# Batched attention and MLP mixer: the last 64 tokens of u with swapped operands, and two transposes moved to ScalarE's queue

## The chip, the core and the metric

The kernel runs on one core of a Trainium2 chip. A core has a matrix engine (TensorE, PE in the tables; PEld is its weight load), VectorE (DVE), ScalarE (ACT), GpSimd (POOL) and SyncE (SP), which here only issues transfers. Each engine works through its own list of instructions in order, and waits on semaphores for the others and for transfers. The time is that of the device in microseconds, from the program's start to its end, lower is better. The profile's span runs from the first to the last recorded instruction and is 1.8 us shorter here.

## The reference

Eight batches, each attention followed by a two-stage mixer:

```python
scores = scale * np.matmul(q, k.transpose(0, 1, 3, 2))        # 8 heads, 576 tokens, 64 wide
scores = np.where(masks[None, :, :, :], scores, -1000000000.0)
...
x = np.ascontiguousarray(attn_out.transpose(0, 2, 1, 3)).reshape(B, S, H * D)
...
xt = x.transpose(0, 2, 1)
h = np.maximum(xt @ w_tok1, 0.0) @ w_tok2
u = x + h.transpose(0, 2, 1)
h2 = np.maximum(u @ w_ch1, 0.0) @ w_ch2
return (u + h2).astype(np.float32)
```

Heads 0 to 3 see the last 32 tokens, heads 4 to 7 every fourth of the last 128, so that scores are computed in bands. x has 576 tokens by 512 channels; the token stage goes 576 to 256 to 576, the channel stage 512 to 1536 to 512. 576 is four blocks of 128 tokens and a tail of 64, and the change is about the tail.

## The kernel before

The loop over batches (L1167) makes one iteration a batch. In iteration b the generator `gen_main(b)` emits the channel stage of batch b, and between its pieces `interleave` (L975) puts a list of steps, sorted by a time that is written by hand beside each: t is advanced by the costs that the pieces and steps give, and a step is emitted when its time is reached. The order in which instructions are emitted is the order on each engine; nothing is reordered later. The steps of iteration b are, for batch b + 1, the last attention products (`value_steps`, matmuls av, VectorE scales them into xn = x), the token stage's hidden layer (`mix_steps`, tiles h1, written `h` in the tables) and u; for batch b + 2 the scores and their exponentials on ScalarE (attp, attd, attt; two groups of heads, group 0 and group 1, `scores_twin`, exponentials L547), their masks on GpSimd, and the transposes of q and k by DMA from SP (tt, kr, qt; L353); for batch b + 3 the loads on SP (L192, L198, later the v loads).

The main line: `gp` matmuls (L934) of u's transpose with the first channel weights, relu by ScalarE into `gt`; then `gen_out`, which makes the output products yx and yw (L778) by a seven-product scheme, with sums of gt tiles on VectorE (`gate_sums`, L737), adds u (`with_u`, L793) and further products (`with_t`, L798), and stores. Batches are paired for their tails: the 64 tail tokens of an even batch and of the odd batch after it share one tile of 128 and are worked through in the odd iteration (`gp_tails`, gt L925; `tails` in `gen_out`, L744 to L755).

u has four forms from batch 2 on. Its blocks of 128 tokens are made in iteration b - 1 by `emit_u` (L640): matmuls of w_tok2's columns with h1 and an add of x on VectorE (L655). A DMA transpose from SP, `uT_dma` (L702), turns all four blocks into utm. ScalarE copies the second half of that into utd in natural order (`uT_place`, L863), for the gp matmuls. Late in iteration b a second DMA transpose, `u_natural` (L708, u<-utd), turns utd back over into u's second half, which `with_u` needs for the last products. The tail is made by `emit_u(b, 4)` (L659 to L664): two matmuls of 128x512 of which only 64 rows are used, and an add of 64x512 into u16t; in odd batches from 3 on another transpose from SP turns the pair of tails over into utt (L700).

PSUM banks are handed out by name, three "fl", three "main" and two "sc", each in turn; a matmul into a bank waits for the reader of what was in it before. Transfers issued from SP and ScalarE are counted on eight lanes of semaphores (DMAHW0 to DMAHW7) in rotation: a transfer that waits for a lane raises the same lane when it has landed.

Of the kernel before, what the change touches and what calls it, by code (L numbers as in the profile page):

```python
# [68 lines left out]
def kernel(  # L69
# [90 lines left out]
    uTt = fixed("utt", [128, 4, 128])  # L160
# [129 lines left out]
    xn, u16w, uT, uT0 = {}, {}, {}, {}  # L290
    gta = fixed("gt", [128, NMB, GW])
    u16t = [fixed(f"u16t{i}", [128, 4, 128]) for i in range(2)] * 2
# [347 lines left out]
    def emit_u(b, s, h1):  # L640
# [15 lines left out]
        else:  # L656
# [6 lines left out]
            t = u16t[b // 2]  # L663
            nc.vector.tensor_tensor(out=t[rows], in0=blocks4(p[rows]), in1=blocks4(xn[b][rows, 4]), op=ALU.add)  # L664

    def emit_uT(b, cb):
        odd = b % 2
        p = bank("fl" if cb % 2 == (cb > 1 if b else 0) else "main", 3, f"tpu_{b}_{cb}", FP16)
# [8 lines left out]
        if cb < 2:  # L677
# [3 lines left out]
            if odd:  # L681
                nc.tensor.transpose(out=p[:, 0:128], in_=u16t[b // 2][:, cb], identity=ident)
            copy(eng, t, p[:, 0:512 + m0])
        else:
# [4 lines left out]
            if odd:  # L689
                nc.tensor.transpose(out=grid[:, :, 0:32], in_=u16t[b // 2][:, cb], identity=perm)  # L690
# [3 lines left out]
    def turned(b):  # L694
        return b >= 2

    def uT_dma(b, tail):
        i = b % 2
        if tail:
            nc.sync.dma_start_transpose(out=uTt, in_=u16t[b // 2].rearrange("p x c -> p (x c)"))  # L700
        else:
            nc.sync.dma_start_transpose(out=uTm[i].rearrange("p x s t -> p (x s) t"),  # L702
                                        in_=u16w[b].rearrange("p x s c -> p (x s c)"))

    def u_natural(b):
        u = u16w[b]
        if turned(b):
            nc.sync.dma_start_transpose(out=u[:, 2:4].rearrange("p x s c -> p (x s) c"),  # L708
                                        in_=uTd.rearrange("p x t -> p (x t)"))
            return  # L710
# [28 lines left out]
    def gen_out(b):  # L739
# [4 lines left out]
        def tails():  # L744
# [7 lines left out]
            nc.vector.tensor_tensor(out=blocks4(o32), in0=blocks4(p), in1=u16t[b // 2], op=ALU.add)  # L752
# [6 lines left out]
        gate_sums(b, 1, (2, 1, 4) if ahead else (2,))  # L759
        if odd and not last:  # L760
# [3 lines left out]
            yield from tail  # L764
        else:
# [90 lines left out]
    def uT_place(b, cb):  # L856
        i = b % 2
        tail = uTt[:, cb]
# [36 lines left out]
    def mix_steps(b, t_h1, t_h1b, t_u, t_uT, du=1.0, turn=6.0, gap=2.6):  # L895
        h1 = [sb.tile([128, DM], FP16, tag="h1", bufs=4, name=f"h1_{b}_{jb}") for jb in range(2)]
# [4 lines left out]
        for i, s in enumerate((4, 0, 1, 2, 3)):  # L901
            steps.append((t_u + du * i, 0.44, lambda s=s: emit_u(b, s, h1)))
        if turned(b):
            for t, tail in ((turn, False), (turn + 1.0, True))[:1 + b % 2]:
                steps.append((t_u + t * du, 0.0, lambda tail=tail: uT_dma(b, tail)))
# [7 lines left out]
    def gen_main(b):  # L913
# [17 lines left out]
        for mb in range(NMB):  # L931
# [13 lines left out]
            if b and mb == (11 if b == 1 else 10):  # L945
                gate_sums(b, 0, (2, 1, 4) if odd and b + 1 < B else (2, 1))
# [153 lines left out]
    def u_half(s, half):  # L1100
# [3 lines left out]
        t = (u16t[0] if s == 4 else u16(0, s))[:, 2 * half:2 * half + 2]  # L1104
# [146 lines left out]
```

## Time and profile before

| | before |
|---|---|
| median of 3 runs | 278.54 us (277.87 to 278.73) |
| the profiled execution: its time | 278.42 us |
| the profiled execution: span | 276.6 us |
| DMA moved | 55.50 MB, mean 201 GB/s |
| DMA transposes, us to landing: kr, qt | 3.6, 3.4 |
| DMA transposes, us to landing: tt, utm | 4.3, 4.6 |
| DMA transposes, us to landing: u<-utd, utt | 3.8, 2.8 |

All times to landing are medians from issue. In the page, a line of section 5 gives the source line, engine, operation, tiles and their sizes, the count, then busy time, mean duration in ns and the idle time ahead of it with what ended it. In the list of waits a row names who waited, for whom, the sum in us, how often, and the longest. In a timeline a row gives the start, the duration, engine, line, operation and tiles, and how many instructions stand together; a bracket holds the idle time ahead of it and who ended it; an engine with a q behind it (SPq, ACTq) is its queue issuing transfers. Iteration 2 ends near 130 us, iteration 4 near 190 and iteration 5 near 222.

### The profile page before, as it was taken

Reading aid. Unit: us, or ns where it says so; the run is one execution under the profiler, and the core shown is the slowest. Engines: PE = TensorE matmul, PEld = TensorE weight load, DVE = VectorE, ACT = ScalarE, POOL = GpSimd, SP = SyncE. Lnnn points to the kernel's source line nnn. Section 1 sums busy time; section 2 is a strip of 40 time slices with the busy share of each in tenths; the row PEclk is TensorE's granted clock in tenths of the full one; section 3 lists DMA queues with packets and bytes.
Section 4 is the critical chain, followed back from the end, with each engine's and each line's share of the span. In section 5 each row is a group of like instructions: output and inputs, shape, how many; then the busy total and the mean of one; then the engine's idle time right before and its main releaser. Section 6 shows DMA issues by size and latency. Waiting matters only on the chain.

```text
span 276.6 us, 6790 instructions
## 1 busy us (share of the span) xinstructions
PE 265.8 (96%) x2694; PEld 197.2 (71%) x2694; DVE 168.3 (61%) x340; ACT 149.0 (54%) x291; POOL 158.8 (57%) x214
## 2 busy tenths in 40 slices
PE   6899999999999999997999999999999999999994
PEld 2796676897666876685775876687776866786673
DVE  6767668575568655674649454775475473961363
ACT  2864774363674465467545656476546565236500
POOL 7880760389858759849973589739980870000000
PEclk9999999999999999999999999999999999999999
DMA  7999999995979799999999999989999220553015
GB/s 216 271 248 238 291 241 210 316 241 159 343 132 226 151 316 281 233 165 259 304 221 186 257 280 255 172 156 316 304 211 148 81 79 2 99 147 78 0 40 152
DMA packets 116783, 55.50 MB, mean 201 GB/s; under 512 B 84976, under 2 KB 115696, under 8 KB 116752
## 3 DMA queue, kind: packets, MB, share of 16 engines
q1 hardware_dynamic: 112096, 49.63, 75.9%
q0 software_dynamic: 2640, 3.94, 7.9%
q10 hardware_dynamic: 2016, 1.51, 1.8%
q8 instruction: 21, 0.34, 0.5%
q14 instruction: 10, 0.08, 0.1%
HBM read 38.12 MB, written 9.44 MB: 172 GB/s over the span
## 4 chain that ended last, share of the span: by engine, by line
PE 85%; DMA 7%; DVE 4%; issue 1%; ACT 1%; ACTq 0%; POOL 0%; DVEq 0%
PE gp L934 29%; PE yx L778 12%; PE yw L778 9%; PE h1p L637 5%; PE up L649 4%; PE gt L925 4%; PE yp L961 4%; PE yp L747 3%; DMA lt<-in_k_dram 3%; PE sc L522 3%; DMA u<-utd 2%; DMA w1p<-in_moe_w_tok_dram 2%; PE h1p L635 1%; PE av L614 1%; PE av L619 1%; DVE gt L737 1%
## 5 line engine op out<-in xcount | busy, mean ns | idle before, releaser
L109 ACT ACTIVATE gt<-gp 128x512 f16<-128x512 f32 x89 | 53.2, 598 | 50.4 <-PE gp L934 50.1
L778 PEld LDWEIGHTS <-gt 128*128 128x128 f16 x600 | 57.0, 98 | 10.2 <-issue 2.0
L934 PE MATMUL gp<-utd,w 128*128 128x512 f16 x144 | 54.7, 380 | 0.0
L934 PE MATMUL gp<-utm,w 128*128 128x512 f16 x144 | 54.6, 379 | 0.0
L934 PEld LDWEIGHTS <-w 128*128 128x128 f16 x384 | 39.1, 113 | 19.8 <-issue 0.5
L115 POOL TENSOR_TENSOR attp<-attp,const 128x1280 f16<-128x1280 f16 x12 | 31.6, 2637 | 23.4 <-ACT attp L547 23.4
L737 DVE TENSOR_TENSOR gt<-gt 128x768 f16<-128x768 f16 x56 | 32.2, 605 | 12.5 <-ACT gt L109 12.2
L115 DVE TENSOR_TENSOR xn<-av,rec 128x320 f16<-128x320 f32 x64 | 31.4, 491 | 2.2
L115 POOL TENSOR_TENSOR attd<-attd,const 128x1024 f16<-128x1024 f16 x12 | 25.5, 2124 | 7.7 <-issue 5.4
L934 PE MATMUL gp<-uT,w 128*128 128x512 f16 x96 | 25.8, 380 | 0.0
L793 DVE TENSOR_TENSOR o<-yx,u 128x512 f32<-128x512 f32 x22 | 15.2, 689 | 11.2 <-PE yx L778 10.5
L778 PE MATMUL yx<-w,gt 128*128 128x256 f16 x168 | 20.6, 273 | 0.0
L778 PE MATMUL yx<-wsum_a,gt 128*128 128x256 f16 x168 | 20.6, 273 | 0.0
L547 ACT ACTIVATE attp<-sc 128x480 f16<-128x480 f32 (+1 forms) x36 | 15.9, 538 | 8.7 <-PE sc L522 8.7
L655 DVE TENSOR_TENSOR u<-up,xn 128x512 f16<-128x512 f32 x26 | 17.8, 688 | 4.1 <-PE up L649 4.1
L626 DVE RECIPROCAL rec<-av 128x5 f32<-128x5 f32 x64 | 12.2, 191 | 12.2 <-PE av L623 12.1
L105 POOL CAST c_k<-l_k 128x512 f16<-128x512 f32 x29 | 17.6, 616 | 2.2 <-DMA l_k<-in_k_dram 1.3
L863 ACT COPY utd<-utm 128x512 f16<-128x512 f16 x12 | 12.7, 1129 | 10.3 <-DMA u<-utd 6.6
L105 POOL CAST c_q<-l_q 128x512 f16<-128x512 f32 x26 | 16.3, 630 | 2.9 <-DMA l_q<-in_q_dram 2.2
L664 DVE TENSOR_TENSOR u16t<-up,xn 64x512 f16<-64x512 f32 x7 | 4.8, 689 | 21.0 <-PE up L660 21.0
L109 ACT ACTIVATE h<-h1p 128x256 f16<-128x256 f32 x31 | 11.8, 384 | 8.9 <-PE h1p L637 8.4
L798 DVE TENSOR_TENSOR o<-yw,o 128x512 f32<-128x512 f32 x13 | 9.0, 691 | 11.4 <-PE yw L778 11.3
(158 smaller groups left out, 549.6 us busy)
## 6 DMA issues: line engine op xcount, KB each, us to landing
l_q<-in_q_dram SPq DMA_DIRECT2D x15, 512.0 KB, 6.6
l_k<-in_k_dram SPq DMA_DIRECT2D x14, 512.0 KB, 7.4
out_dram<-o SPq DMA_DIRECT2D x26, 256.0 KB, 4.1
l_vn<-in_v_dram SPq DMA_DIRECT2D x32, 128.0 KB, 6.7
l_vd<-in_v_dram SPq DMA_DIRECT2D x16, 256.0 KB, 4.2
w<-in_moe_w_ch_dram POOLq DMA_DIRECT2D x6, 512.0 KB, 7.6
out_dram<-o SPq DMA_DIRECT2D x17, 128.0 KB, 2.7
l_vt<-in_v_dram SPq DMA_DIRECT2D x8, 256.0 KB, 4.7
```

What stands on the lines that cost most here:

```text
L105: eng.tensor_copy(out=out, in_=in_)
L109: nc.scalar.activation(out=out, in_=in_, func=AF.Relu)
L115: eng.tensor_tensor(out=out, in0=x, in1=y, op=ALU.mult)
L547: nc.scalar.activation(out=out, in_=in_, func=AF.Exp, scale=0.125)
L626: nc.vector.reciprocal(out=rec[:, :, 0], in_=av[:, :, 64])
L637: nc.tensor.matmul(out=p, lhsT=w[:, s, j], rhs=x[:, s, c], start=False, stop=(s == 3))
L655: nc.vector.tensor_tensor(out=u16(b, s), in0=blocks4(p), in1=blocks4(xn[b][:, s]), op=ALU.add)
L737: nc.vector.tensor_tensor(out=out, in0=x, in1=y, op=op)
L778: nc.tensor.matmul(out=p, lhsT=gta[:, k0 + mb, r:r + 128], rhs=weights[:, mb, c], start=(first and not mb and (not a or len(parts) > 2)), ...
L793: nc.vector.tensor_tensor(out=grid(o[(i, j)]), in0=grid(p), in1=u, op=ALU.add)
L863: nc.scalar.copy(out=natural(uTd[:, cb - 2]), in_=uTm[i][:, cb].rearrange("p r m -> p m r"))
L934: nc.tensor.matmul(out=p, lhsT=w3_block(cb, mb), rhs=uT[(b, cb)][0], start=(i == 0), stop=(i == 3))
```

## The change

From batch 2 on the tail of u is no longer made in iteration b - 1 but in iteration b, at t = 1.6, by a new function `emit_u_tail`. It swaps the operands: h1 is the stationary side and the 64 columns of w_tok2 the moving one, so that the result is already transposed: four blocks of 128 channels by 64 tokens, eight matmuls of 128x64 and one add of 128x256. The add needs x's last block transposed, xtt, which a DMA transpose from ScalarE's queue makes in iteration b - 1 (`turn_x`). In odd batches SP turns the pair of tails over into u16t at t = 2.6 (`turn_tails`), the other way round than before; there are two utt and one u16t now.

The transpose u<-utd of batches 2 to 5 is issued from ScalarE's queue at t = 17.3 (19.7 in odd iterations) in place of SP's at 14.6 (15.0); in batches 6 and 7 it stays. `uT_dma` comes 1.0 steps of u earlier relative to u's blocks. In batch 1 one transposed tile takes a bank "fl" in place of "main" (`emit_uT`), and gate sum 4 stands behind the add of the tails in iterations 1, 3 and 5 (group 1) and 1 (group 0).

```diff
--- before.py
+++ after.py
@@ -157,7 +157,8 @@
     w4 = [w4a[:, i] for i in range(NMB)]
     idle = fixed("idle", [128, 512])
     uTm = [fixed(f"utm{i}", [128, 4, 4, 128]) for i in range(2)]
-    uTt = fixed("utt", [128, 4, 128])
+    uTt = [fixed(f"utt{i}", [128, 4, 128]) for i in range(2)]
+    xTt = fixed("xtt", [128, 4, 128])
     uTd = fixed("utd", [128, 2, 512])
 
     def emit_fixed():
@@ -287,9 +288,9 @@
         return steps
 
 
-    xn, u16w, uT, uT0 = {}, {}, {}, {}
+    xn, u16w, uT, uT0, h1s = {}, {}, {}, {}, {}
     gta = fixed("gt", [128, NMB, GW])
-    u16t = [fixed(f"u16t{i}", [128, 4, 128]) for i in range(2)] * 2
+    u16t = fixed("u16t", [128, 4, 128])
 
     def u16(b, s):
         if b not in u16w:
@@ -660,12 +661,12 @@
                 nc.tensor.matmul(out=p, lhsT=w2[jb][:, c0:c0 + 128], rhs=h1[jb],
                                  start=(jb == 0), stop=(jb == 1))
             rows = slice(64, 128) if odd else slice(0, 64)
-            t = u16t[b // 2]
+            t = u16t
             nc.vector.tensor_tensor(out=t[rows], in0=blocks4(p[rows]), in1=blocks4(xn[b][rows, 4]), op=ALU.add)
 
     def emit_uT(b, cb):
         odd = b % 2
-        p = bank("fl" if cb % 2 == (cb > 1 if b else 0) else "main", 3, f"tpu_{b}_{cb}", FP16)
+        p = bank("fl" if (cb != 2 if b else cb % 2 == 0) else "main", 3, f"tpu_{b}_{cb}", FP16)
         if odd:
             t = sb.tile([128, 640], FP16, tag="ut1", bufs=4, name=f"uT_{b}_{cb}")
         else:
@@ -679,7 +680,7 @@
                 nc.tensor.transpose(out=p[:, m0 + 128 * s:m0 + 128 * s + 128],
                                     in_=u16(b, s)[:, cb], identity=ident)
             if odd:
-                nc.tensor.transpose(out=p[:, 0:128], in_=u16t[b // 2][:, cb], identity=ident)
+                nc.tensor.transpose(out=p[:, 0:128], in_=u16t[:, cb], identity=ident)
             copy(eng, t, p[:, 0:512 + m0])
         else:
             grid = p[:, 0:4 * RS].rearrange("p (r i) -> p r i", i=RS)
@@ -687,25 +688,37 @@
             for s in range(4):
                 nc.tensor.transpose(out=grid[:, s, m0:m0 + 128], in_=u16(b, s)[:, cb], identity=ident)
             if odd:
-                nc.tensor.transpose(out=grid[:, :, 0:32], in_=u16t[b // 2][:, cb], identity=perm)
+                nc.tensor.transpose(out=grid[:, :, 0:32], in_=u16t[:, cb], identity=perm)
             copy(eng, natural(t), grid[:, :, 0:128 + m0].rearrange("p r m -> p m r"))
         uT[(b, cb)] = (t[:, 128:640], t[:, 0:128]) if odd else (t, None)
 
     def turned(b):
         return b >= 2
 
-    def uT_dma(b, tail):
+    def uT_dma(b):
         i = b % 2
-        if tail:
-            nc.sync.dma_start_transpose(out=uTt, in_=u16t[b // 2].rearrange("p x c -> p (x c)"))
-        else:
-            nc.sync.dma_start_transpose(out=uTm[i].rearrange("p x s t -> p (x s) t"),
-                                        in_=u16w[b].rearrange("p x s c -> p (x s c)"))
-
-    def u_natural(b):
+        nc.sync.dma_start_transpose(out=uTm[i].rearrange("p x s t -> p (x s) t"),
+                                    in_=u16w[b].rearrange("p x s c -> p (x s c)"))
+
+    def turn_x(b):
+        nc.scalar.dma_start_transpose(out=xTt, in_=xn[b][:, 4])
+
+    def turn_tails(b):
+        nc.sync.dma_start_transpose(out=u16t, in_=uTt[b // 2 % 2].rearrange("p x t -> p (x t)"))
+
+    def emit_u_tail(b):
+        p = bank("fl", 3, f"up_{b}_4")[:, 0:256].rearrange("p (x t) -> p x t", t=64)
+        for cb in range(4):
+            for jb in range(2):
+                nc.tensor.matmul(out=p[:, cb], lhsT=h1s[b][jb][:, 128 * cb:128 * cb + 128], rhs=w2[jb][:, 512:S],
+                                 start=(jb == 0), stop=(jb == 1))
+        t = slice(64 * (b % 2), 64 * (b % 2) + 64)
+        nc.vector.tensor_tensor(out=uTt[b // 2 % 2][:, :, t], in0=p, in1=xTt[:, :, t], op=ALU.add)
+
+    def u_natural(b, queue=nc.sync):
         u = u16w[b]
         if turned(b):
-            nc.sync.dma_start_transpose(out=u[:, 2:4].rearrange("p x s c -> p (x s) c"),
+            queue.dma_start_transpose(out=u[:, 2:4].rearrange("p x s c -> p (x s) c"),
                                         in_=uTd.rearrange("p x t -> p (x t)"))
             return
         for cb in (2, 3):
@@ -749,19 +762,22 @@
                 if mb in (3, 7):
                     yield 0.87
             o32 = sb.tile([128, DM], FP32, tag="o32", bufs=4, name=f"o32_{b}_4")
-            nc.vector.tensor_tensor(out=blocks4(o32), in0=blocks4(p), in1=u16t[b // 2], op=ALU.add)
+            nc.vector.tensor_tensor(out=blocks4(o32), in0=blocks4(p), in1=u16t, op=ALU.add)
             nc.sync.dma_start(out=out[b - 1, 512:S, :], in_=o32[0:64])
             nc.sync.dma_start(out=out[b, 512:S, :], in_=o32[64:128])
             yield 0.87
 
         base = turn["main"]
         ahead = odd and not last
-        gate_sums(b, 1, (2, 1, 4) if ahead else (2,))
+        gate_sums(b, 1, (2, 1) if ahead else (2,))
         if odd and not last:
             tail = tails()
             yield next(tail)
             spare.append(base)
             yield from tail
+            if b == 1:
+                gate_sums(b, 0, (4,))
+            gate_sums(b, 1, (4,))
         else:
             spare.append(base)
         turn["main"] = base + 2
@@ -855,7 +871,7 @@
 
     def uT_place(b, cb):
         i = b % 2
-        tail = uTt[:, cb]
+        tail = uTt[b // 2 % 2][:, cb]
         if cb < 2:
             uT[(b, cb)] = (uTm[i][:, cb].rearrange("p s t -> p (s t)"), tail)
         else:
@@ -893,16 +909,15 @@
         return steps
 
     def mix_steps(b, t_h1, t_h1b, t_u, t_uT, du=1.0, turn=6.0, gap=2.6):
-        h1 = [sb.tile([128, DM], FP16, tag="h1", bufs=4, name=f"h1_{b}_{jb}") for jb in range(2)]
+        h1 = h1s[b] = [sb.tile([128, DM], FP16, tag="h1", bufs=4, name=f"h1_{b}_{jb}") for jb in range(2)]
         steps = []
         for half, at in ((0, t_h1), (1, t_h1b)):
             for jb in range(2):
                 steps.append((at + 0.9 * jb, 0.55, lambda jb=jb, half=half: emit_h1(b, jb, half, h1[jb])))
-        for i, s in enumerate((4, 0, 1, 2, 3)):
+        for i, s in enumerate((0, 1, 2, 3) if turned(b) else (4, 0, 1, 2, 3)):
             steps.append((t_u + du * i, 0.44, lambda s=s: emit_u(b, s, h1)))
         if turned(b):
-            for t, tail in ((turn, False), (turn + 1.0, True))[:1 + b % 2]:
-                steps.append((t_u + t * du, 0.0, lambda tail=tail: uT_dma(b, tail)))
+            steps.append((t_u + turn * du, 0.0, lambda: uT_dma(b)))
             for t, cb in ((0.0, 2), (0.0, 0), (gap, 3), (gap, 1)):
                 steps.append((t_uT + t, 0.0, lambda cb=cb: uT_place(b, cb)))
         else:
@@ -943,7 +958,7 @@
                 for g in range(2):
                     gate_sums(b, g, (3,))
             if b and mb == (11 if b == 1 else 10):
-                gate_sums(b, 0, (2, 1, 4) if odd and b + 1 < B else (2, 1))
+                gate_sums(b, 0, (2, 1, 4) if odd and 1 < b < B - 1 else (2, 1))
         if b:
             yield from gen_out(b)
             return
@@ -1181,11 +1196,11 @@
             steps += scores2[:10]
             steps += at(34.0, 0.0, [lambda: emit_loads_qk(3)])
         elif b == 1:
-            steps += at(13.5, 0.0, [lambda: u_natural(1)])
+            steps += at(13.5, 0.0, [lambda: u_natural(1)]) + at(24.0, 0.0, [lambda: turn_x(2)])
             va = value_steps(2, 0.0, 1.0)
             steps += [(0.8 + 0.4 * i, c, f) for i, (_, c, f) in enumerate(scores2[10:])]
             steps += [(t, c, f) for t, (_, c, f) in zip((2.2, 3.0, 4.8, 5.6, 8.2, 9.0, 10.4, 11.2), va)]
-            steps += mix_steps(2, 7.0, 13.0, 15.1, 24.6, 1.0, 5.6, 0.8)
+            steps += mix_steps(2, 7.0, 13.0, 15.6, 24.6, 1.0, 5.1, 0.8)
             casts = cast_steps(3)
             steps += [(6.0 + 0.5 * i, 0.0, casts[i]) for i in (0, 2, 4, 6, 8)]
             steps += [(9.5 + 1.0 * i, 0.0, lambda i=i: cast_qk(3, "q", i, nc.scalar)) for i in range(4)]
@@ -1204,12 +1219,19 @@
             steps += at(11.0, 0.3, casts[9:14]) + at(12.5, 0.0, [places[i] for i in (0, 1, 4)])
             steps += at(13.0, 0.3, casts[14:16]) + at(14.0, 0.0, places[2:4]) + at(14.2, 0.0, casts[16:])
         else:
-            late = 2.4 * (b % 2)
-            steps += at(14.6 + late / 6, 0.0, [lambda b=b: u_natural(b)])
+            odd = b % 2
+            late = 2.4 * odd
+            if b + 1 < B:
+                steps += at(23.2 if odd else 20.4, 0.0, [lambda b=b: turn_x(b + 1)])
+            steps += at(1.6, 0.25, [lambda b=b: emit_u_tail(b)])
+            if odd:
+                steps += at(2.6, 0.0, [lambda b=b: turn_tails(b)])
+            steps += at(14.6 + late / 6 if b + 2 >= B else 17.3 + late, 0.0,
+                        [lambda b=b: u_natural(b, nc.sync if b + 2 >= B else nc.scalar)])
             if b + 1 < B:
                 va = value_steps(b + 1, 0.4, 0.95)
                 steps += va[:6] + [(t + late / 5, c, f) for t, c, f in va[6:]] + mix_steps(
-                    b + 1, 5.4 + late / 6, 8.2 + late / 6, 10.6 + late / 6, 22.4 + late, 0.9, 4.1, 1.0)
+                    b + 1, 5.4 + late / 6, 8.2 + late / 6, 10.6 + late / 6, 22.4 + late, 0.9, 3.1, 1.0)
             if b + 2 < B:
                 steps += at(2.0, 0.6, cast_steps(b + 2)) + score_steps(b + 2, 21.4 if b % 2 else 18.0, 8.4 if b % 2 else 6.4)
                 places = place_steps(b + 2)
```

Three places in the order of the program follow, before and after. A row has the source line, the operation, tile written and tiles read, size, and the semaphores that it waits for; PE_49, DVE_49, Pool_49 and Activation_49 are the engines' own.

The first is ScalarE in iteration 2, from the copy of k's last part (kt) to the copies into utd; sc_0 are the scores of group 0. Before:

```order
L103 COPY kt<-kr 128x512 [waits DMAHW7_49,Pool_49]
L547 ACTIVATE attp<-sc_0_5_2193 128x2x128 [waits PE_49,Activation_49,Pool_49]
L547 ACTIVATE attt<-sc_0_5_2193 128x2x64 [waits Activation_49]
...
L547 ACTIVATE attp<-sc_0_4_2192 128x2x128 [waits Activation_49]
L547 ACTIVATE attt<-sc_0_4_2192 128x2x64 [waits Activation_49]
L863 COPY utd<-utm_90 128x512 [waits DMAHW4_49,DMAHW3_49,Activation_49]
```

and with the change:

```order
L103 COPY kt<-kr 128x512 [waits DMAHW0_49,Pool_49]
L721 DMA_TRANSPOSE u_2_1640<-utd 128x8x128 [waits DMAHW4_49,DMAHW3_49,DMAHW6_49,DMAHW2_49,DMAHW7_49,DMAHW1_49,Activation_49]
L548 ACTIVATE attp<-sc_0_5_2196 128x2x128 [waits PE_49,Pool_49]
L548 ACTIVATE attt<-sc_0_5_2196 128x2x64
...
L548 ACTIVATE attp<-sc_0_4_2195 128x2x128
L548 ACTIVATE attt<-sc_0_4_2195 128x2x64
L704 DMA_TRANSPOSE xtt<-xn_1904 128x4x128 [waits DMAHW5_49,DVE_49]
L879 COPY utd<-utm_90 128x512 [waits DMAHW6_49]
```

Two transposes have come into the queue, one ahead of group 0's exponentials and one ahead of the copies. The first of them waits for lanes 1, 2, 3, 4, 6 and 7.

The second is SP in the same iteration, from the transposes of batch 4's k and q to batch 5's loads. Before:

```order
L353 DMA_TRANSPOSE kr<-c_k_1962 128x8x128 [waits DMAHW7_49,Pool_49]
L353 DMA_TRANSPOSE qt<-c_q_1957 128x8x128 [waits DMAHW0_49]
L353 DMA_TRANSPOSE kr<-c_k_1962 128x8x128 [waits DMAHW1_49,Pool_49]
L353 DMA_TRANSPOSE qt<-c_q_1957 128x8x128 [waits DMAHW2_49]
L702 DMA_TRANSPOSE utm_90<-u_3_2104 128x16x128 [waits DMAHW3_49,DVE_49]
L708 DMA_TRANSPOSE u_2_1643<-utd 128x8x128 [waits DMAHW4_49,Activation_49]
L700 DMA_TRANSPOSE utt<-u16t_95 128x4x128 [waits DMAHW5_49]
L198 DMA lt_2176<-in_q_dram 64x8x64 [waits DMAHW6_49]
```

and with the change:

```order
L354 DMA_TRANSPOSE kr<-c_k_1970 128x8x128 [waits DMAHW0_49,Pool_49]
L354 DMA_TRANSPOSE qt<-c_q_1965 128x8x128 [waits DMAHW1_49]
L354 DMA_TRANSPOSE kr<-c_k_1970 128x8x128 [waits DMAHW2_49,Pool_49]
L354 DMA_TRANSPOSE qt<-c_q_1965 128x8x128 [waits DMAHW3_49]
L700 DMA_TRANSPOSE utm_90<-u_3_2102 128x16x128 [waits DMAHW4_49,DVE_49]
L199 DMA lt_2189<-in_q_dram 64x8x64 [waits DMAHW5_49]
L199 DMA lt_2189<-in_k_dram 64x8x64 [waits DMAHW7_49]
```

Two transposes behind utm are gone, and lt comes next. The lanes of kr, qt, kr, qt and utm are now 0 to 4; lanes 1 to 4 are among those for which ScalarE's u<-utd waits, at the values that these very transfers raise, and lane 7 is that of tt just ahead of them.

The third is PE with the tail, up_4. Before, that of batch 3 in iteration 2, between gp_7 and gp_8:

```order
L934 LDWEIGHTS w_1_85
L934 MATMUL gp_7_2082<-utm_89,w_1_85 128x512
L660 LDWEIGHTS w_81
L660 MATMUL up_4_2089<-h_3_0_1901,w_81 128x512
L660 LDWEIGHTS w_81
L660 MATMUL up_4_2089<-h_3_1_1902,w_81 128x512
L934 LDWEIGHTS w_2_86
L934 MATMUL gp_8_2096<-utd,w_2_86 128x512
```

and with the change that of batch 2 in the same iteration, behind the second head's values matmuls:

```order
L624 LDWEIGHTS attt
L624 MATMUL av_1_1923<-vv_70,attt 128x65
L713 LDWEIGHTS h_2_0_1317
L713 MATMUL up_4_1935<-w_81,h_2_0_1317 128x64
L713 LDWEIGHTS h_2_1_1318
L713 MATMUL up_4_1935<-w_81,h_2_1_1318 128x64
...
L949 LDWEIGHTS w_0_84
L949 MATMUL gp_1_1920<-utd,w_0_84 128x512
```

Batch 3's two matmuls of 512 columns have gone from iteration 2 (its tail comes in iteration 3), and batch 2's eight of 64 columns, of which two are shown, have come to its start; before, batch 2's tail stood in iteration 1.

More of the change, by code (lines that the diff above doesn't have):

```diff
@@ L1103, in u_half @@
         rows = slice(0, 64) if s == 4 else slice(0, 128)
-        t = (u16t[0] if s == 4 else u16(0, s))[:, 2 * half:2 * half + 2]
+        t = (u16t if s == 4 else u16(0, s))[:, 2 * half:2 * half + 2]
         summed = s in (0, 2)
```

## The prediction, made before the changed kernel ran

> **What bounds the kernel now.** I began with the page's busy times and the chain that ended last.
>
> ```profile
> PE 265.8 (96%) x2694; PEld 197.2 (71%) x2694; DVE 168.3 (61%) x340; ACT 149.0 (54%) x291; POOL 158.8 (57%) x214
> PEclk9999999999999999999999999999999999999999
> PE 85%; DMA 7%; DVE 4%; issue 1%; ACT 1%; ACTq 0%; POOL 0%; DVEq 0%
> ```
>
> TensorE (PE) works 96% of the span at full clock and carries the end: a microsecond of its work removed is worth a microsecond, until somebody makes it wait. So I next read the list of waits for the places where PE already waits.
>
> ```profile
> PE yw L778 <- DVE o L793: 1.5, 1, 1.5
> PE yp L961 <- DVE o L967: 0.4, 1, 0.4
> PE yw L778 <- DVE o L752: 0.2, 1, 0.2
> ```
>
> These three (2.1 us) are the steady state's waits for another engine that the change touches. The longest is followed back in the chain, cut to iteration 2:
>
> ```profile
> 119.61 5.71 DMA u<-utd
> ...
> 125.44 0.70 DVE o L793
> ...
> 126.18 0.81 PE yw L778 x6
> ```
>
> SP issues u's turned half (u<-utd) at 119.61, it lands 5.71 later, VectorE adds it and PE goes on. That is the DMA that the change hands to ScalarE. So the third view is SP's own timeline in iterations 2 and 4, with the landing times of utm, the transfer ahead of it.
>
> ```profile
> 115.98 1.33 SPq L353 DMA_TRANSPOSE qt<-c_q  x1
> 117.41 2.11 SPq L702 DMA_TRANSPOSE utm<-u  x1
> 119.61 1.69 SPq L708 DMA_TRANSPOSE u<-utd  x1
> ...
> 175.28 1.34 SPq L353 DMA_TRANSPOSE qt<-c_q  x1
> 177.81 1.32 SPq L702 DMA_TRANSPOSE utm<-u  x1
> ```
>
> ```profile
> utm<-u SPq DMA_TRANSPOSE x1, 6.3
> utm<-u SPq DMA_TRANSPOSE x1, 4.3
> DMA to landing us min/median/max: 3.2/3.8/5.7
> ```
>
> The first two rows are utm's times to landing in iterations 2 and 4, so utm lands at 117.41 + 6.30 = 123.71 and at 177.81 + 4.30 = 182.11. The third row is u<-utd, over six. In iteration 2 u<-utd is issued while utm is still under way.
>
> **The change, part by part.** *The tail on PE.* For the price of a 128x512 matmul and of a matmul with some 64 columns I take PE's timeline at the end of iteration 2.
>
> ```profile
> 129.79 0.38 PE L934 MATMUL gp<-utm,w 128*128 128x512 f16 x1
> 130.01 0.19 PE L614 MATMUL av<-vv,attp 128*128 128x65 f16 x1
> 130.04 0.20 PE L612 MATMUL av<-vv,attp 128*128 128x65 f16 x1
> ...
> 130.25 0.39 PE L934 MATMUL gp<-utd,w 128*128 128x512 f16 x1
> ```
>
> The starts give the pace: 0.22 for 128x512, and (130.25 - 130.01) / 8 = 0.03 for 128x65, each with a weight load of its own. Two of the former go in each of six batches (0.43), eight of 128x64 come (0.24): -0.19 each, -1.1 in all. VectorE's add changes from 64x512 to 128x256; neither is on the path.
>
> *The two short waits.* The other bank takes away the 0.4, and the moved gate sums the 0.2, with nothing late behind them that I can see: -0.6.
>
> *What ScalarE's queue now waits for.* The order of the changed program shows that ScalarE's u<-utd waits for the landing of every transpose that SP has issued before, utm of the next batch the last of them. No row of before has such a wait, since all its transposes are SP's. ScalarE works in order, so everything behind it waits too: the exponentials of group 0, x's turned block (another issue), the two copies into utd, and the exponentials of group 1. Their prices are in ScalarE's timeline of iteration 2.
>
> ```profile
> 117.89 1.09 ACT L103 COPY kt<-kr 128x512 f16<-128x512 f16 x1
> 120.16 0.38 ACT L547 ACTIVATE attp<-sc 128x256 f16<-128x256 f32 x1 [1.19 <-PE sc L522]
> ...
> 122.66 0.35 ACT L547 ACTIVATE attt<-sc 128x128 f16<-128x128 f32 x1
> 125.41 2.08 ACT L863 COPY utd<-utm 128x512 f16<-128x512 f16 x2 [2.40 <-DMA u<-utd]
> 127.79 0.66 ACT L547 ACTIVATE attt<-sc 128x256 f16<-128x256 f32 x2 [0.30 <-PE sc L522]
> 128.33 2.08 ACT L547 ACTIVATE attd<-sc 128x512 f16<-128x512 f32 x4
> ```
>
> Group 0 takes 122.66 + 0.35 - 120.16 = 2.85, the copies 2.08. The next iteration's first values matmul (av, 130.01) takes a bank that the third of group 1's last four exponentials frees: 128.33 + 3/4 x 2.08 = 129.89, only 0.12 before it. From the group's start at 127.79 to av it is 2.22. That small slack is why the delay reaches PE.
>
> An issue of a transpose from ScalarE's queue stands nowhere in the trace. Bounds: SP's issues of a transpose are quoted above from 1.32 to 2.11, ScalarE's issue of a plain load is
>
> ```profile
> 1.80 0.71 ACTq L198 DMA_DIRECT2D lt<-in_k_dram  x1
> ```
>
> I take 1.3, SP's short case, since ScalarE will have waited until the transposes are through, and keep 0.7 and 2.1 as ends. From utm's landing to the first av of the next iteration it is then 1.3 + 2.85 + 1.3 + 2.08 + 2.22 = 9.75.
>
> Iteration 2: utm lands at 123.71, av would start at 133.46 instead of 130.01: **+3.45**. The wait for u's half is inside it: landing 123.71 + 3.8 = 127.5, add 0.7, PE at 128.2, then the 3.83 of PE work from 126.18 to 130.01 gives 132.0, still earlier than ScalarE. With utm at 4.3, as in iteration 4, it would be +1.45.
>
> Iteration 4, from the same timeline there:
>
> ```profile
> 187.58 0.66 ACT L547 ACTIVATE attt<-sc 128x256 f16<-128x256 f32 x2 [1.19 <-PE sc L522]
> ```
>
> Its first av stands at 187.58 + 2.22 = 189.80. utm can go earlier here: the tail's step ahead of u's slabs is gone and its turn comes sooner, while SP is free at 175.28 + 1.34 = 176.62; I take 176.9, between that and 177.81. It lands at 181.2, and 181.2 + 9.75 = 190.95: **+1.15**.
>
> Odd iterations, in number 5, by SP's issue of utm, its time to landing and ScalarE's timeline:
>
> ```profile
> 206.12 2.93 SPq L702 DMA_TRANSPOSE utm<-u  x1
> ```
>
> ```profile
> utm<-u SPq DMA_TRANSPOSE x1, 6.1
> ```
>
> ```profile
> 212.21 0.38 ACT L547 ACTIVATE attp<-sc 128x256 f16<-128x256 f32 x1 [1.81 <-PE sc L522]
> ...
> 220.17 0.66 ACT L547 ACTIVATE attt<-sc 128x256 f16<-128x256 f32 x2 [3.14 <-PE sc L522]
> ```
>
> utm lands at 212.2, just as group 0 starts, so the wait itself costs nothing, and ScalarE idles 3.14 before group 1, more than the two issues (2.6): nothing is late. Without that cover they would cost what iteration 4 costs. In 6 and 7 u's half stays on SP: nothing. In iteration 1 ScalarE waits only with x's block; the copies behind it need utm anyway.
>
> What is saved ahead of iteration 2's utm (both short waits, 0.6, batch 2's tail, 0.43, batch 3's net of batch 2's new one, 0.19) is 1.2 at most. SP, whose issues stand end to end there (115.98 + 1.33 to 117.41), sets utm: bounds 0 and -1.2, I take -0.5. Behind iteration 2 there remain four tails out (1.72) and five in (1.2): -0.5. SP loses four issues, and six more small transposes run; no row of before prices either on this path, and I put both at 0, between a utm that lands 2.0 sooner and one that lands 2.0 later (its two times), an end each that the range keeps.
>
> **Sum**, against the profiled execution's own 278.42 (span 276.6 and 1.8 around it, 0.12 below the median of 278.54): 278.42 + 3.45 + 1.15 - 0.5 - 0.5 = **282.0**.
>
> On the trace's own rows alone the wait would not be needed: SP issued u<-utd 6.30 - 2.20 = 4.1 before utm had landed. The Trainium skill, "DMA: Bandwidth & Descriptors", section "Silent corruption: two transposing streams in flight at once", says that transposes issued from SP and from ScalarE are two streams, and that the later one's first transpose must wait for the full completion of the earlier. By that rule the moved DMA costs what is summed here; without it the first rival's 275.2 would follow. No run so far can show it, as before has one such stream.
>
> **The rivals.** *Faster (275.2).* The wait is covered: utm lands before ScalarE needs the exponentials. Then the tails (-1.1), the short waits (-0.6) and the 1.5 behind u's half all go: 278.4 - 3.2. It decides at one point: landing plus issue by 120.16, where group 0 starts now, hence utm issued at 115.16 or before, 2.25 earlier than now, even with 4.3 to landing and 0.7 an issue. For it: ScalarE idles 1.19 there, and 2.40 before the copies. Against it: SP's issues stand end to end.
>
> *No net change (278.6).* utm goes out 0.8 earlier in iteration 2 and needs 4.3: landing 120.9, av at 130.65, +0.65, with what is saved ahead of it already inside; in iteration 4 a short issue (0.7) makes it fit; -0.5 behind. For it: 4.3 is the shorter of two measured times. Against: PE's saving ahead of it reaches SP only in part.
>
> *Much slower (287.3).* An issue takes ScalarE 2.1 as well. That adds 1.6 in each of iterations 2 and 4, and in 3 and 5 two issues are 4.2 against 3.14 of idle time, 1.1 each: 282.0 + 3.2 + 2.1. It decides from 1.57 an issue, where the odd iterations lose their cover. For it: SP's issue of utm in iteration 2 took as much. Against: that was with another transpose in flight, which ScalarE's issue will not have beside it.
>
> **How the numbers follow.** Forecast 0.58, faster 0.18, no change 0.14, much slower 0.10. The forecast's own range: utm at 4.3 in iteration 2 alone gives 280.0, issues of 0.7 alone give 282.0 - 1.2 - 1.15 = 279.6, and utm at 6.3 in iteration 4 as well gives 284.0; so 279.6 to 284.0. The range of 277.0 to 284.8, which takes in most issues between 1.3 and 2.1, leaves out 0.13 of the faster case and 0.07 of the much slower one. A measurement of this kernel tells 0.3% from no change, so the bounds are 277.7 and 279.4. Faster: 0.16 of the first rival and 0.02 of the second, 0.18. Same: 0.02, 0.10 and 0.03 of the forecast, 0.15. Slower: 0.55, 0.10 and 0.02, 0.67.
>
> **What would show it.** Right: in iteration 2 ScalarE has a gap of some 5 us between the kt copy and group 0, ended by utm; PE waits before the first av of iterations 3 and 5, for ScalarE, and not in 4 and 6; the waits of 0.4 and 0.2 are gone; each tail's matmuls take about 0.24. Wrong: group 0 starts within 1.5 us of the kt copy, or utm lands before 120. What would make the prediction wrong is above all utm's landing in iterations 2 and 4, one trace's 6.3 and 4.3, and an issue from ScalarE far from 1.3.

## The result and the profile after

The changed kernel takes 291.84 us in the median of six runs (289.75 to 294.87), the kernel before 278.56; the ratio is 1.0468 with a 95% interval of 1.0418 to 1.0517. The medians are over all executions; the ratios and intervals, here and below, leave out those in a slower state that the kernel before shows too. The direction was right, but the time lies far above the range of 277.0 to 284.8. The profiled execution took 291.44, with a span of 289.6: 13.0 more than the 276.6 of before.

The page of the changed kernel, the lines that answer to those of before:

```profile
PE 266.1 (92%) x2730; PEld 197.8 (68%) x2730; DVE 167.8 (58%) x340; ACT 148.8 (51%) x291; POOL 157.5 (54%) x214
PEclk9999999999999999965899999999999999999999
PE 80%; DMA 12%; DVE 3%; SPq 1%; ACT 1%; issue 1%; ACTq 0%; DVEq 0%
```

PE's busy time is as before (266.1 against 265.8), its share is lower: nearly all of the 13 us is time in which PE waits. The clock, level before, has a dip at three slices in the middle. The list of waits names the place:

```profile
PE yw L794 <- DVE o L809: 15.0, 2, 12.6
...
DVE o L809 <- DMA l_q<-in_q_dram: 13.3, 1, 13.3
...
DVE o L809 <- DMA u<-utd: 3.0, 1, 3.0
```

PE waits 15.0 for the add of u's half (L809 is L793 of before) in two places, where before it waited 1.5 in one. The short waits of 0.4 and 0.2 are gone. For VectorE's long wait ahead of that add the list names an l_q load as the releaser. That load landed within 0.1 us of u<-utd, and the add reads u; the timelines of iteration 2 show it, SP's first, then ScalarE's, then VectorE's:

```profile
118.25 3.20 SPq L700 DMA_TRANSPOSE utm<-u  x1
121.51 0.67 SPq L199 DMA_DIRECT2D lt<-in_q_dram  x1
122.23 0.65 SPq L199 DMA_DIRECT2D lt<-in_k_dram  x1
122.92 0.78 SPq L193 DMA_DIRECT2D l_q<-in_q_dram  x1
123.81 0.44 SPq L822 DMA_DIRECT2D out_dram<-o  x1
124.29 0.47 SPq L193 DMA_DIRECT2D l_k<-in_k_dram  x1
124.80 0.66 SPq L193 DMA_DIRECT2D l_q<-in_q_dram  x1
125.51 1.58 SPq L193 DMA_DIRECT2D l_k<-in_k_dram  x1
```

```profile
116.61 1.07 ACT L103 COPY kt<-kr 128x512 f16<-128x512 f16 x1
124.89 2.13 ACTq L721 DMA_TRANSPOSE u<-utd  x1
127.12 0.39 ACT L548 ACTIVATE attp<-sc 128x256 f16<-128x256 f32 x1 [9.43 <-issue]
...
127.40 1.33 ACTq L704 DMA_TRANSPOSE xtt<-xn  x1
...
135.21 2.04 ACT L879 COPY utd<-utm 128x512 f16<-128x512 f16 x2 [5.24 <-DMA u<-utd]
```

```profile
135.31 0.69 DVE L809 TENSOR_TENSOR o<-yw,u 128x512 f32<-128x512 f32 x1 [13.30 <-DMA l_q<-in_q_dram]
```

utm needs 6.4 and lands at 124.64; 0.25 later ScalarE issues u<-utd. The wait is there, as the order of the program said. But u<-utd then takes 10.3 to land, where SP's took 3.8 in the median and 5.7 in this iteration. Its times to landing in iterations 2, 3, 4 and 5 of the changed kernel:

```profile
u<-utd ACTq DMA_TRANSPOSE x1, 10.3
...
u<-utd ACTq DMA_TRANSPOSE x1, 7.7
...
u<-utd ACTq DMA_TRANSPOSE x1, 5.6
...
u<-utd ACTq DMA_TRANSPOSE x1, 3.1
```

In iterations 2 to 4 SP issues loads of batch b + 3 around it, in iteration 5 there are none left, and 3.1 is as fast as SP's fastest.

The windows around the long wait show the clock (the columns are the stretch, its length, then busy time by engine, the granted clock, the DMA share and GB/s):

```profile
123.30:125.30 2.00, 0.13 (x2) 0.00 (x0) 0.00 (x0) 0.00 (x0) 0.00 (x0) 1.00 1.01 148
...
126.50:136.05 9.55, 0.00 (x0) 0.00 (x0) 0.69 (x1) 3.69 (x9) 5.78 (x3) 0.50 1.07 265
136.05:139.80 3.75, 3.75 (x37) 2.63 (x37) 1.38 (x2) 1.20 (x2) 0.00 (x0) 0.54 0.66 169
139.80:141.00 1.20, 1.20 (x14) 1.08 (x13) 0.00 (x0) 1.06 (x3) 0.00 (x0) 1.00 0.60 172
```

From 126.50 on the DMA engines are full during the wait. PE's clock falls to half, and when the data comes PE runs 3.75 us at 0.54: 1.7 us more. The account is 15.0 - 1.5 of waits for u's half, + 1.7 for the clock, - 0.6 for the short waits, - 1.1 for the tails (this last is the prediction's estimate): 13.5, against 13.0 measured.

### The profile page after: what moved, and what is told of

The parts are those of the page before. It is cut to its first block, busy times and chain, and to the rows that moved or that the text cites. A ratio compares the mean times of both kernels' runs of the same rounds, so it can differ in the third digit from the quotient of the medians.

```text
span 289.6 us, 6886 instructions
## 1 busy us (share of the span) xinstructions
PE 266.1 (92%) x2730; PEld 197.8 (68%) x2730; DVE 167.8 (58%) x340; ACT 148.8 (51%) x291; POOL 157.5 (54%) x214
## 4 chain that ended last, share of the span: by engine, by line
PE 80%; DMA 12%; DVE 3%; SPq 1%; ACT 1%; issue 1%; ACTq 0%; DVEq 0%
PE gp L949 27%; PE yx L794 11%; PE yw L794 8%; PE h1p L638 5%; PE up L650 4%; PE gt L940 4%; PE yp L976 4%; PE yp L760 4%; DMA l_q<-in_q_dram 4%; PE sc L523 3%; DMA lt<-in_k_dram 2%; DMA l_vt<-in_v_dram 2%; DMA u<-utd 2%; DMA utm<-u 2%; PE h1p L636 1%; PE av L620 1%
## 5 line engine op out<-in xcount | busy, mean ns | idle before, releaser
L750 DVE TENSOR_TENSOR gt<-gt 128x768 f16<-128x768 f16 x56 | 34.0, 629 | 12.1 <-ACT gt L109 11.6
L794 PE MATMUL yw<-wsum_b,gt 128*128 128x256 f16 x72 | 10.1, 296 | 15.0 <-DVE o L809 15.0
L809 DVE TENSOR_TENSOR o<-yx,u 128x512 f32<-128x512 f32 x22 | 15.2, 690 | 14.7 <-PE yx L794 14.4
L809 DVE TENSOR_TENSOR o<-yw,u 128x512 f32<-128x512 f32 x6 | 4.1, 692 | 18.3 <-DMA l_q<-in_q_dram 13.3
```

The source lines that it names most:

```text
L750: nc.vector.tensor_tensor(out=out, in0=x, in1=y, op=op)
L794: nc.tensor.matmul(out=p, lhsT=gta[:, k0 + mb, r:r + 128], rhs=weights[:, mb, c], start=(first and not mb and (not a or len(parts) > 2)), ...
L809: nc.vector.tensor_tensor(out=grid(o[(i, j)]), in0=grid(p), in1=u, op=ALU.add)
```

## The experiments

Three theories stood at the start. **A**: u<-utd goes out late, behind utm's landing, and then shares the DMA engines with loads that SP no longer holds back. **B**: a transpose is slow on ScalarE's queue as such. **C**: the new tail and the transposes of x cost the time. Edits are against the changed kernel unless said otherwise. Some kernels ran only once; there the time says little, and the trace of that run is what is read.

**u<-utd back on SP.**

```diff
-            steps += at(14.6 + late / 6 if b + 2 >= B else 17.3 + late, 0.0,
-                        [lambda b=b: u_natural(b, nc.sync if b + 2 >= B else nc.scalar)])
+            steps += at(14.6 + late / 6, 0.0, [lambda b=b: u_natural(b)])
```

> The changed kernel, with u<-utd of batches 2 to 5 issued by SP again, right behind utm; x's block stays with ScalarE. Theory A (u<-utd lands late because it starts only when utm has landed, and then shares the DMA engines with the loads that SP no longer holds back): u<-utd goes out by 121.5 and lands within 6 us of its issue in iteration 2, PE's stall there falls from 12.8 to between 2.5 and 5, that of 2.5 in iteration 4 goes, and the time is 277 to 281. Theory B (a transpose from ScalarE's queue is slow in itself): the same, 277 to 281. Theory C (the new tail and the transposes of x cost the time): above 286.

Measured: 279.13, beside 279.37 for the kernel before on the same chip; ratio 1.000, interval 0.9953 to 1.0046. u<-utd is issued at 120.46 and needs 5.8. The list of waits of this run, its one row of PE for u's half:

```profile
PE yw L794 <- DVE o L809: 1.9, 1, 1.9
```

The wait is below A's 2.5 to 5, that of iteration 4 is gone. Behind x's block, still on ScalarE, PE waits 0.8 ahead of iteration 2. The whole loss hangs on the move of u<-utd; C has fallen as its cause. What is left of the change gains nothing that can be measured either.

**The move alone, in the kernel before.** `u_natural` there gets the changed kernel's queue and time; tail, bank and gate sums stay.

> The kernel before, with u<-utd of batches 2 to 5 alone moved to ScalarE's queue, at the changed kernel's time; tail, banks and gate sums as before. Theory A (late start behind SP's transposes, then loads in flight): the move alone costs what the change cost. In iteration 2 u<-utd waits for utm and for utt behind it, goes out at 124 to 126 and takes 7 us or more to land; PE stalls there for 8 us or more; 286 to 295. Theory C (the new tail and x's transposes have a part in it): under 284.

Measured in a single run: 297.21. u<-utd waits for utt too, goes out at 125.34 and takes 9.1; 7.2, 7.5 and 3.1 in iterations 3 to 5. Its PE waits:

```profile
PE yw L778 <- DVE o L793: 15.6, 2, 10.5
```

The move alone costs about as much as the whole change. The time is above what A expected, and one run can't say by how much; the mechanism is A's. B still stood.

**The loads later.**

```diff
-                steps += at(17.6, 0.9, load_steps(b + 3))
+                steps += at(24.3 if b in (2, 4) else 17.6, 0.9, load_steps(b + 3))
```

> The changed kernel, with u<-utd on ScalarE, but the loads of batch b + 3 emitted at 24.3 instead of 17.6 in iterations 2 and 4, so that SP issues them behind a store that needs u's half. Theory A: u<-utd goes out with utm's landing as before, near 124.9, but lands 3 to 4.5 us after its issue instead of 10.3 (iteration 2) and 5.6 (iteration 4); PE's stalls fall from 12.8 to some 5.6 to 7 and from 2.5 to under 1; 281 to 285 if the later loads cost nothing. Theory B: still some 10 us to landing, 289 or more.

Measured in a single run: 292.88. Time to landing of u<-utd in iterations 2, 3 and 4:

```profile
u<-utd ACTq DMA_TRANSPOSE x1, 3.1
...
u<-utd ACTq DMA_TRANSPOSE x1, 9.5
...
u<-utd ACTq DMA_TRANSPOSE x1, 4.2
```

In iterations 2 and 4, where the loads were held back, it is 3.1 and 4.2 in place of 10.3 and 5.6; in iteration 3, where the loads stand as in the change, 9.5. PE's wait in iteration 2 fell to 3.2 us, and its longest now stands in iteration 3 (6.9 us), so the total did not fall, which A's 281 to 285 had not foreseen; why iteration 3 lost its cover was not tried. B has fallen: the same queue is fast without loads beside it.

**The same loads ahead, on SP.** All transposes on SP, u<-utd in iterations 2 and 4 behind the first loads. The lines on u<-utd and on x's block are shown; the steps of x's block move as well, to 21.3 in iterations 2 and 4.

```diff
+            steps += at(14.6 + late / 6 if b + 2 >= B else 21.2 if b in (2, 4) else 14.6 + late / 6, 0.0,
+                        [lambda b=b: u_natural(b, nc.sync)])
-        nc.scalar.dma_start_transpose(out=xTt, in_=xn[b][:, 4])
+        nc.sync.dma_start_transpose(out=xTt, in_=xn[b][:, 4])
```

> The changed kernel with all transposes on SP, so that none waits for another queue, and u<-utd and x's block at 21.2 in iterations 2 and 4, where SP has issued two lt, l_q and l_k loads before. Theory A: what is under way sets the time to landing, whichever queue issues: u<-utd takes 7 us or more in iteration 2, where 3.7 was measured on SP ahead of the loads. Theory B (ScalarE's queue is served worse than SP's): 5 us or less.

Measured in a single run: 291.46. u<-utd is issued at 124.91 and needs 6.8 in iteration 2 and 5.9 in iteration 4; PE waits 13.6 for u's half, 9.0 of it in iteration 2. The time is that of the changed kernel, with no transpose on ScalarE at all. The 6.8 is short of A's 7 by a little and above B's 5: behind the loads SP's queue is slow as well, but not by 10.3.

**The first four loads alone ahead, on ScalarE.** It asks what makes the difference between 6.8 and 10.3.

```diff
-                steps += at(17.6, 0.9, load_steps(b + 3))
+                ls = load_steps(b + 3)
+                steps += at(17.6, 0.9, ls[:4]) + at(24.3, 0.5, ls[4:]) if b in (2, 4) else at(17.6, 0.9, ls)
```

> The changed kernel, u<-utd on ScalarE; in iterations 2 and 4 the first four loads (two lt, l_q, l_k) go out as in the change, ahead of u<-utd, and the other ten only behind a store that needs u's half. It splits the 10.3 us to landing. Theory A1 (u<-utd shares the DMA engines with the loads under way when it is issued, and, since it sits in a queue of its own, with those that SP issues after it as well): without the later loads it takes 6 to 8 us in iteration 2, as on SP behind the same four (6.8), and PE's stall is 8 to 10. Theory A2 (only what is ahead counts, and ScalarE's queue gets the smaller share of it): still 9.5 us or more.

Measured in a single run: 7.0 to landing, PE's wait 7.4, a little under the expected 8. The run's time of 300.18 says nothing, since in this run PE also waited 5.7 for GpSimd's vt near 51 us, ahead of the first edited iteration. With the same four loads, ScalarE's queue takes as long as SP's. The other 3.3 us go with the loads that SP issues at the same time or later: behind u<-utd on SP's own queue they stand after it, beside ScalarE's queue they share the engines with it. The packets show the sharing. Below are what SP's queue (q1) and ScalarE's (q10) moved while ScalarE's two transposes (u<-utd and xtt, 256 and 128 KB) ran, in packets, MB and share of the 16 engines, first from 128.8 to 135.2 in the changed kernel, then from 137.5 to 140.3 in this run:

```profile
q1 hardware_dynamic: 1194, 1.18, 76.5%
q10 hardware_dynamic: 1422, 0.35, 37.2%
...
q10 hardware_dynamic: 1598, 0.39, 95.1%
q1 hardware_dynamic: 221, 0.21, 22.0%
```

In both runs the first of these packets comes some 4 us behind the issue (3.9 and 4.2), where the run with all loads later has 1.2; the rest, 6.4 against 2.8, goes with the sharing. That is A1, on a single run each. Why the packets start so late on a queue of their own was not tried.

**u<-utd late, on SP, x's block on ScalarE.**

```diff
+            steps += at(14.6 + late / 6 if b + 2 >= B else 21.2 if b in (2, 4) else 17.3 + late, 0.0,
+                        [lambda b=b: u_natural(b, nc.sync)])
```

> The changed kernel, with u<-utd on SP, at 21.2 in iterations 2 and 4, so that it goes out behind the two lt, l_q and l_k loads in SP's own queue; ScalarE's wait for utm is gone. Theory A: the loads ahead make it slow on SP too, 7 us or more from issue to landing in iteration 2, PE's stall there 8 us or more. Theory B: 6 us or less, as SP's took before.

Measured in a single run: 295.95, and not the test that it was meant to be. ScalarE issues xtt at 122.70, it needs 7.3, and SP then waits:

```profile
122.26 0.98 SPq L193 DMA_DIRECT2D l_k<-in_k_dram  x1
130.01 1.26 SPq L721 DMA_TRANSPOSE u<-utd  x1
```

SP stood until xtt had landed at 129.96, 6.7 us by its list of waits; u<-utd itself then took 3.2. PE waits 10.8 in iteration 2 and 6.4 in iteration 4. The expectation of 7 failed, because the wait between the two engines' transposes works in both directions, and a small transpose on one queue held the other's for 7 us.

**Everything on SP.** u<-utd at 14.6 and x's block right behind it (at 21.5 in iteration 1); the line that changes x's queue is shown.

```diff
-        nc.scalar.dma_start_transpose(out=xTt, in_=xn[b][:, 4])
+        nc.sync.dma_start_transpose(out=xTt, in_=xn[b][:, 4])
```

> The changed kernel with both kinds of transposes on SP, u<-utd at its old time and x's block right behind it: the tail with swapped operands alone, with its moved gate sums and bank. Theories A and B: 276 to 280, and within 1 us of the run with only u<-utd on SP. Theory C: above 284.

Measured: 280.6, ratio 1.0052 (1.0011 to 1.0092). SP's stream of iteration 2 comes later: utm goes out at 120.72 in place of 118.32, and PE waits 2.7 for u's half in place of 1.9. Of these 2.4, x's block in iteration 1 is 1.3; the rest was there ahead of it in this run.

**u<-utd early.** utd holds its data since the iteration before, so u<-utd may go ahead of q's and k's transposes. Tried on the changed kernel with u<-utd on SP, then with all transposes on SP, and on the kernel before:

```diff
-            steps += at(14.6 + late / 6, 0.0, [lambda b=b: u_natural(b)])
+            steps += at(8.4, 0.0, [lambda b=b: u_natural(b)])
```

> The changed kernel with u<-utd of all batches from 2 on SP at 8.4, ahead of the transposes of q and k (utd holds the batch's data since the iteration before), and x's block on ScalarE as in the change. Theory A: nothing of u's half is late, PE's stall ahead of yw in iteration 2 goes (2.07 in the run with u<-utd at 14.6 on SP), and utm goes out some 1.3 later without a new wait; 275 to 278 by the chip's before of 278.5, so 1 to 3 us below it. A rival: utm 1.3 later makes kt, utd or x's block late, and PE stalls as long as before: within 1 us of before.

Measured: 281.32, ratio 1.0107 (1.0068 to 1.0147). The wait for u's half is gone, and a new one has come, the rival's. The waits of PE, then ScalarE's timeline of iteration 2:

```profile
PE gp L949 <- ACT attt L548: 3.1, 2, 2.0
```

```profile
127.84 1.62 ACTq L704 DMA_TRANSPOSE xtt<-xn  x1
129.50 2.02 ACT L879 COPY utd<-utm 128x512 f16<-128x512 f16 x2 [4.76 <-DMA lt<-in_k_dram]
131.43 0.65 ACT L548 ACTIVATE attt<-sc 128x256 f16<-128x256 f32 x2
```

utm lands at 127.67, x's block is issued right behind it, the copies and group 1 behind that, and PE waits 2.0 at the start of iteration 3, and 1.0 at the start of iteration 2 in the same way. It is the chain that the prediction had summed, with the smaller transpose in it. In the profiled run PE also ran at half clock for 3.4 us right behind the 2.0, some 1.7 us more.

> The changed kernel with all transposes on SP and u<-utd at 8.4, ahead of those of q and k: the tail with swapped operands with no transpose from ScalarE's queue and no late half of u. If the rest of the change saves PE what it should (1.1 of matmuls and the two short waits), 276 to 278, 0.5 to 2 us below before. If the six more transposes on SP's queue eat it (they push SP's stream in iterations 1 and 2, and kt and utm are late), 279 or more.

Measured: 281.46, ratio 1.0088 (1.0041 to 1.0135). With x's block on SP no ScalarE wait is left, but PE waits 1.9 for qt late in iteration 2: SP's stream is late. Behind that wait, too, 3.4 us run at half clock in the profiled run, and 1.4 more is a wait for VectorE in iteration 4 whose cause was not looked for. This fits the expectation that the six more transposes eat what the tail saves; no run separates them from the rest.

> The kernel before with u<-utd at 8.4 on SP and nothing else changed. Theory A: the 1.5 to 1.6 us of wait for u's half in iteration 2 goes, the rest stays: 0.5 to 1.6 us below before. A rival: utm lands 1.3 later and ScalarE's copies, then group 1, hold PE up at the end of iteration 2 by 1 us or more: no gain.

Measured: 277.53 beside 278.53, ratio 0.9993 (0.9963 to 1.0022). In its profile PE's wait for u's half is gone and the span is 275.1, but the timed runs can't tell it from no change.

**The small parts alone, in the kernel before**: u<-utd at 8.4, the bank, the moved gate sums.

> The kernel before with three of the small parts and none of the large ones: u<-utd at 8.4 on SP, the other bank in emit_uT, the moved gate sums. The three waits of PE (1.5 or 1.6, 0.4 or 0.5, 0.2 or 0.4) go, PE never waits behind 40 us: 276 to 277.5, 1 to 2.5 us below before. A rival: the gate sums come too late elsewhere, or before's gain stays lost in its spread: within 0.5 us.

Measured: 279.95, ratio 1.0056 (1.0018 to 1.0094), a miss. The three waits are gone, and one of 2.1 has come in their place, for VectorE ahead of yx in iteration 1, where two of the moved gate sums took 3.45 us in the profiled run (1.02 in the changed kernel). Why they were slow there was not tried.

**On ScalarE, but early.** u<-utd at 1.0 in place of 17.3.

```diff
-            steps += at(14.6 + late / 6 if b + 2 >= B else 17.3 + late, 0.0,
+            steps += at(14.6 + late / 6 if b + 2 >= B else 1.0, 0.0,
```

> The changed kernel with u<-utd of batches 2 to 5 still on ScalarE, but at 1.0 in place of 17.3 (19.7), ahead of SP's transposes of the same iteration, so that it waits for none of them in flight; x's block stays where the change has it. Theory A (not the queue but the place costs: behind utm's landing, beside the loads): PE's waits for u's half go in all iterations, even if u<-utd lands slowly; what is left is x's block, which holds ScalarE until utm has landed and then delays group 1, some 1 to 3 us ahead of iteration 3 as with u<-utd early on SP: 279 to 283. Theory B (ScalarE's queue itself): 287 or more.

Measured: 282.1, ratio 1.0135 (1.0042 to 1.0228). u<-utd takes up to 7.8 beside the loads, and PE never waits for u's half. What is left are waits for ScalarE:

```profile
PE gp L949 <- ACT attt L548: 2.9, 2, 1.7
...
PE gp L949 <- ACT gt L109: 1.3, 1, 1.3
```

Those for attt (1.1 and 1.7, ahead of iterations 2 and 3) stand behind x's block. The 1.3 is in iteration 4 and stands behind u<-utd itself: ScalarE issued it only at 169.40, behind the landing of an l_vn load, and so relu into gt came late; in iteration 3 the same cost 0.9, behind xtt's landing. So u<-utd did wait for transfers in flight, though not for SP's transposes. Still, some ten of the 13 us go without taking u<-utd off ScalarE's queue. It was the place.

## Why the prediction was wrong

**The step that failed** is u<-utd's time to landing, "landing 123.71 + 3.8 = 127.5", and with it the removed issues: "SP loses four issues, and six more small transposes run; [...] I put both at 0". The 3.8 is the median of transposes that stood ahead of the loads. It measured 10.3, so that u's half landed at 135.18: 6.5 us in one term. In iteration 4 the same term was 5.6 and made a wait of 2.4. The order of u<-utd and the loads was turned round: u<-utd went from 119.61 to 124.89, and with u<-utd and utt out of SP's queue lt went out at 121.51 in place of 123.12 and all four l_q and l_k loads by 125.51. The removed issues are 1.6 of that, the late start 5.3. The prediction's own row of iteration 2, 5.71, would already have put u's half behind ScalarE's chain: 123.71 + 5.71 + 0.7 + 3.83 = 133.95, against 133.46.

**Right was the wait itself.** ScalarE's gap between the kt copy and group 0 was 9.43, where some 5 had been forecast, ended by utm and the issue. The program does keep transposes from two engines apart, and u<-utd went out 0.25 behind utm's landing, 5.3 later than before. The same wait worked against SP too, which the prediction did not think of.

**The chain through ScalarE (+3.45, +1.15) was real but covered.** No wait of PE for ScalarE stands ahead of iteration 3 or 5 in the changed kernel, against what "What would show it" said, because PE came 12.6 late itself. Where u's half was not late, it showed: 2.0 at the end of iteration 2 with x's block alone. And it showed at the end of iteration 1, which had been put at nothing, in four other runs (0.8 to 1.4), though not in the changed kernel's own trace: the issue there stands between utm's landing and the copies.

**The issue from ScalarE**, taken as 1.3, was 1.25 three times of four for u<-utd and 2.13 in iteration 2, 1.2 to 1.4 for x's block. The "much slower" rival had the right sign by the wrong cause.

**The odd iterations** cost nothing, as said, though in iteration 3 u<-utd took 7.7: the cover was there. **The tails and the two short waits** went as forecast: eight matmuls of 128x64 take 0.23 (101.46 to 101.69), against 0.24, and the waits of 0.4 and 0.2 are gone. The part saved ahead of utm (0.5) can't be read from one trace: utm of iteration 2 went out at 118.25 in the changed kernel, 0.84 later than before, but at 117.07 and 116.56 in the runs with later loads and with u<-utd late on SP, which are the same program up to there. In the schedule, uT_dma and u's blocks moved together, one step of u earlier in the iteration; against each other they kept their places in batches 3 to 7, other than said under "The change".

**Not foreseen was the clock**, 1.7 us of it. In the changed kernel PE idles from 123.43, and its clock falls to half 2.5 us later. The length of one wait does not decide it. In the run with later loads it fell near the end of a wait of 3.2. After the wait of 2.4 in iteration 4 of the changed kernel, and after one of 2.7 in the run with everything on SP, it kept 1.00. But in the run with u<-utd early on SP a wait of 2.0 was followed by 3.41 us at half clock:

```profile
129.82:131.86 2.04, 0.00 (x2) 0.00 (x0) 0.69 (x1) 2.04 (x4) 0.84 (x1) 1.00 1.08 380
132.10:135.51 3.41, 3.41 (x31) 2.04 (x30) 0.88 (x3) 2.49 (x5) 2.32 (x2) 0.50 1.16 206
```

With all transposes on SP and u<-utd early it was 3.41 us again, behind a wait of 1.9. The Trainium skill, "TensorE: Matmul & The Clock Gate", in "Part 1: The HAM clock gate", gives an idle window of about 3.4 us for that. The half-clock stretch of 3.41 us has that length, but the waits ahead of it were shorter than such a window, so a wait below 3.4 us is no safe one here.

## What to carry to other kernels

A transfer that is taken out of a queue is also the thing that held back whatever stood behind it: price the move by the times to landing that stand where it goes, with the loads that are then in flight, and not by its own times from the old place. In this program two queues that both transpose are one queue with waits between them, in both directions, and the engine that issues also stops computing for the wait (9.43 us of ScalarE's here). Where the data is ready an iteration earlier, an earlier place helps more than another queue: u<-utd at 1.0 on ScalarE cost 9.7 us less than at 17.3, though that is still 3.0 above the kernel before on the same chip.

## What the runs showed of the hardware

A DMA transpose of 256 KB took 3.1 us with no load beside it and 10.3 with two l_q and two l_k loads of 512 KB issued within 3 us of it; with two lt, one l_q and one l_k ahead of it, 6.8 on SP's queue, and 7.0 on ScalarE's with the later loads held back. The Trainium skill, "DMA: Bandwidth & Descriptors", in "Issuing engines are not separate DMA queues", says that transfers from all engines run on the same 16 DMA engines and interleave; these runs agree: while ScalarE's transposes moved 0.35 MB, SP's loads moved 1.18 MB. They add that a transfer in a queue of its own shares the engines with later loads, which on one queue stand behind it.

No version tried beats the kernel before by more than can be measured.
